# Six products for one extra row of a Fourier transform, with its low half in column 32 of the high operand; two real parts ahead in layer 0

## The chip, the cores and the metric

The kernel runs on one core of a Trainium2 chip. The metric is the device time of one launch in microseconds (us). A core has a matrix engine (TensorE, PE in the profile; PEld is its loading of the stationary operand), VectorE (DVE), ScalarE (ACT), GpSimd (POOL) and SyncE (SP, which here issues the DMAs). Each engine works off its own queue of instructions in order; engines wait for each other through semaphores.

## What is computed

Two layers, each a Fourier mixing and then a linear attention, both on the layer norm of the residual stream `x` (2048 tokens of 640, fp32):

```python
def _A_ref(x, dft_seq_re, dft_seq_im, dft_hid_re, dft_hid_im):
    a = jnp.einsum("bsd,ed->bse", x, dft_hid_re)
    b = jnp.einsum("bsd,ed->bse", x, dft_hid_im)
    y = jnp.einsum("ts,bse->bte", dft_seq_re, a) - jnp.einsum("ts,bse->bte", dft_seq_im, b)
    return y

def _B_ref(x, wqkv, wo):
    ...
    phi = lambda t: jnp.where(t > 0, t + 1, jnp.exp(t)) + 1e-6
    pq, pk = phi(q), phi(k)
    kv = jnp.einsum("bhsd,bhse->bhde", pk, v)
    z = jnp.einsum("bhsd->bhd", pk)
    num = jnp.einsum("bhqd,bhde->bhqe", pq, kv)
    den = jnp.einsum("bhqd,bhd->bhq", pq, z)[..., None] + 1e-6
    ...

x = x + _A_ref(_layernorm(x, axis=-1), ...)
x = x + _B_ref(_layernorm(x, axis=-1), B_wqkv, B_wo)
x = x + _A_ref(_layernorm(x, axis=-1), ...)
x = x + _B_ref(_layernorm(x, axis=-1), B_wqkv, B_wo)
```

There are 32 heads of width 20. The time depends on shapes alone.

## The kernel before

**Numbers in pairs.** TensorE multiplies here in fp32r, a rounded form of fp32. To keep fp32's precision, every operand is held as a pair: a high half (ScalarE casts it, L183) and a low half (the source minus the high half, L184, on VectorE or GpSimd). A product is then three: high by high, high by low, low by high.

**Fourier.** The transform over the sequence runs first, then the one over the channels. Both use the symmetry of the matrices, so that only real parts over 322 of the 640 channels and half of the sequence rows are multiplied; the rest are sums and differences. The sequence's results are kept by `kept` as pairs of 128x640 tiles, named `u` in the trace and `UT[ci, c]` in the code: `ci` 0 to 2 is the kind of transform, `c` 0 to 2 a chunk of 128 channels. Columns 0 to 511 of a tile are four groups of 128 sequence rows. For `ci == 0` there is one more sequence row, the middle one, t = 1024: column 512. The kernel fills the columns behind it with zeros, since the extra row is multiplied as a stationary operand of 128 columns.

`hidden` multiplies one group of 128 columns by the channel matrix: three chunks by three products, nine in all (L1102). `outputs(par, ahead, mid)` makes the residual's new rows: `par` 1 is the odd sequence rows, 0 the even ones. For each of four groups `r` there is a real part and an imaginary part in one psum buffer (names `ps`; there are four such buffers, and a product waits until the one it is given comes free). `ahead` says how many real parts stand ahead of the first imaginary part. When both parts of a group are done, ScalarE copies the imaginary part (L1129), VectorE makes difference `ym` and sum `yp` (L1130, L1131), and four additions put them into `x`: L1133 on VectorE and L1134 on GpSimd for the lower rows, L1141 and L1142 for the upper ones. In group 0 of the even rows, the extra row comes between: nine products into a psum buffer of its own, `p2`, and two copies (L1138, L1139) that put it into row 0 of `ym` and `yp`, after `ym`'s and `yp`'s old row 0 has been used by L1133 and L1134.

**What stands around it.** `PLANS` gives each layer its order: `o11 … w b q o03t` is, for layer 0, odd rows, sequence transforms, then the key projection's weights (`w`), the first normalized tile (`b`), the query projection's weights (`q`), and the even rows with three real parts ahead (`o03`). The `t` gives `outputs` a `mid` that is called once the first group's imaginary part is issued: it turns the first normalized tile by five transposes on TensorE (L196), into one psum buffer, and splits it (L183, L184). Behind the even rows stands the attention's first pass: the key and query projections (L245), a token tile at a time.

In layer 0 the weights come from memory: each of the 128x640 tiles is loaded by SP into one of four raw buffers, cast on ScalarE (L183) and subtracted (L184) on VectorE, or, for four of the five query tiles, on GpSimd. In layer 1 they are read back ready made. The scheduler sets the order of instructions on each engine, from the program's order, what depends on what, and a table of offsets (`AHEAD`); on each engine the instructions then run in that order.

Of the kernel before, what the change touches and what calls it, by code (L numbers as in the profile page):

```python
# [8 lines left out]
F32 = mybir.dt.float32  # L9
F32R = mybir.dt.float32r  # L10
AF = mybir.ActivationFunctionType
ALU = mybir.AluOpType
# [44 lines left out]
ASTATS = ((4, 10, 11, 13, 14), (1, 4, 8, 10))  # L57
VSTATS = ((4, 7, 13), (1, 2, 6, 7, 8, 13, 15))
RESID = ((4, 4), (3, 3))
PLANS = ('o11 s11 s12 s02 s00 s01 s10 w b q o03t', 's00 o12 s11 s12 s10 s01 s02 b w q o01t')  # L60
COL = (0, 1, 3, 2)
WLOWS = ((4, 0), (1, 1))
PAUSES = (4, 10, 11, 12, 13, 14)
# [955 lines left out]
class Fourier:  # L1019
# [58 lines left out]
    def kept(self, ci, pu, hi, lo, eng):  # L1078
        k, nc = self.k, self.k.nc
        if ci < 2:  # L1080
            woven = lambda t: t[:, :512].rearrange("p (n two) -> p two n", two=2)
            k.split(pu.rearrange("p (two n) -> p two n", two=2)[:, :, :256], woven(hi), woven(lo))
        else:
            nc.scalar.copy(hi[:, :512], pu)
            eng.tensor_tensor(lo[:, :512], pu, hi[:, :512].bitcast(F32), op=ALU.subtract)
        if ci == 0:
            for t in (hi, lo):
                nc.gpsimd.memset(t[:, 514:].bitcast(F32), 0.0)
            k.split(pu[:, 256:258], hi[:, 512:514], lo[:, 512:514])

    def whole(self, T, ci, c):
        pu = self.k.psum()
# [11 lines left out]
    def outputs(self, par, ahead, mid=None):  # L1104

        k, nc, X = self.k, self.k.nc, self.X
        pu = {}

        def real(r):
            if r < 4:  # L1110
                pu[r] = k.psum()
                self.hidden(2 * par, 128 * r, pu[r], 0)

        for r in range(ahead):
            real(r)
        for r in range(4):
            p = pu[r]
            self.hidden(2 * par + 1, 128 * r, p, 512)
            if r == 0 and mid is not None:
                mid()  # L1120
            g, q = 2 * par + r % 2, r // 2
            lo, hi = X[4 * g + q], X[4 * g + 3 - q]
            yi = k.temp(shape=(128, 322))
            ym, yp = k.temp(shape=(128, 322)), k.temp(shape=(128, 322))
            with k.ahead("out", par, r):
                if par:
                    nc.scalar.activation(yi, p[:, 512:834], AF.Copy, scale=k.sign[:, int(r in (1, 2)) :][:, :1])
                else:
                    nc.scalar.copy(yi, p[:, 512:834])  # L1129
                nc.vector.tensor_tensor(ym, p[:, :322], yi, op=ALU.subtract)  # L1130
                nc.vector.tensor_tensor(yp, p[:, :322], yi, op=ALU.add)  # L1131
            with k.ahead("lo", par, r):
                nc.vector.tensor_tensor(lo[:, :HC], lo[:, :HC], ym[:, :HC], op=ALU.add)  # L1133
                nc.gpsimd.tensor_tensor(lo[:, HC:], lo[:, HC:], yp[:, 1:HD], op=ALU.add)  # L1134
            if par == 0 and r == 0:
                p2 = k.psum()
                self.hidden(0, 512, p2, 0)
                nc.vector.tensor_copy(ym[0:1, :], p2[0:1, :322])  # L1138
                nc.vector.tensor_copy(yp[0:1, :], p2[0:1, :322])  # L1139
            with k.ahead("hi", par, r):  # L1140
                k.engine(r < RESID[k.layer][par]).tensor_tensor(hi[:, :HC], hi[:, :HC], yp[:, :HC], op=ALU.add)  # L1141
                nc.gpsimd.tensor_tensor(hi[:, HC:], hi[:, HC:], ym[:, 1:HD], op=ALU.add)  # L1142
            real(r + ahead)
# [17 lines left out]
    def run(self, T, att):  # L1161

        self.work(T, att, PLANS[self.k.layer])

# [370 lines left out]
```

## Time and profile before

| | us |
|---|---|
| median of 3 runs | 749.95 |
| lowest and highest | 749.91, 750.39 |
| profiled execution | 750.25 |
| its span, from first to last instruction | 748.1 |
| mean TensorE clock granted | 1.00 |

The profile is of one execution, on the one core. It is a page and views of its trace: the chain of waits follows the work that ended last back from the end, naming at each step what released it; a timeline gives an engine's instructions with start, duration, number and the idle time before (and what ended it); a group collects the instructions of one line, engine and form, with busy time, mean ns of one, and the idle time of the engine just before them. The names of tiles are written without their numbers. TensorE is busy 726.5 us of the span, VectorE 585.1, ScalarE 374.5, GpSimd 248.9.

Durations overlap a little: an instruction's row reaches into the start of the next of its engine.

### The profile page before, as it was taken

What the parts mean: (1) busy time and instruction counts of PE and PEld (TensorE: products, weight loads), DVE (VectorE), ACT (ScalarE), POOL (GpSimd) and SP (SyncE); (2) the same over time, 40 slices, a digit from 0 to 9 for tenths busy, and PEclk for the clock granted to TensorE, in tenths of its full rate; (3) what the DMA queues carried; (4) which work ended last, traced back from release to release, by engine and by line L of the source; (5) the groups of instructions that cost most, each with busy time, mean ns of one, the idle gap of its engine ahead of it and who ended that gap; (6) DMA issues with size and microseconds to landing.
All of it is one profiled execution on the core that took longest, in us unless ns stands there. A gap on an engine that the chain in (4) does not pass through costs nothing.

```text
span 748.1 us, 12737 instructions
## 1 busy us (share of the span) xinstructions
PE 726.5 (97%) x4734; PEld 690.3 (92%) x4734; DVE 585.1 (78%) x1142; ACT 374.5 (50%) x705; POOL 248.9 (33%) x282
## 2 busy tenths in 40 slices
PE   4999999999999999999999999999999999999997
PEld 1388999999999999899986999999999999989997
DVE  7997798758968786888984756966887886689983
ACT  7745655664355543455773336566532554443320
POOL 5237932120014002567773672026000020154300
PEclk9999999999999999999999999999999999999999
DMA  9322467445665840400043222645265535002553
GB/s 335 97 90 90 128 201 257 126 133 181 187 187 184 283 146 21 151 9 1 11 140 133 70 94 77 222 144 168 59 187 168 164 114 155 23 12 71 178 171 114
DMA packets 55548, 98.78 MB, mean 132 GB/s; under 512 B 5268, under 2 KB 22935, under 8 KB 55479
## 3 DMA queue, kind: packets, MB, share of 16 engines
q1 hardware_dynamic: 55479, 97.89, 41.2%
q8 instruction: 39, 0.64, 0.4%
q14 instruction: 30, 0.25, 0.1%
HBM read 75.84 MB, written 21.63 MB: 130 GB/s over the span
## 4 chain that ended last, share of the span: by engine, by line
PE 80%; DVE 10%; ACT 6%; issue 2%; DMA 1%; POOL 1%; SPq 0%; DVEq 0%; ACTq 0%
PE ps L245 50%; PE ps L338 18%; PE ps L1156 4%; PE ps L1102 4%; PE ps L520 2%; PE ps L196 1%; DVE t L184 1%; PE ps L1061 1%; DVE w L184 1%; ACT t L885 1%; DVE ps L586 1%; DVE x L615 1%; ACT t L886 1%; ACT ab L922 1%; ACT ab L923 1%
## 5 line engine op out<-in xcount | busy, mean ns | idle before, releaser
L245 PE MATMUL ps<-w,t 128*128 128x320 f32 x2880 | 432.4, 310 | 0.5 <-DVE w L184 0.2
L245 PEld LDWEIGHTS ps<-w,t 128*128 128x128 f32 x2880 | 422.9, 188 | 2.0 <-DVE t L184 0.4
L338 PE MATMUL ps<-t,t 128*128 128x256 f32 (+1 forms) x640 | 139.9, 309 | 0.0
L1230 DVE CUSTOM_DVE_ANT_0 junk<-ck,ck 128x688 bf16<-128x688 f32 (+5 forms) x138 | 103.6, 751 | 7.5 <-DMA ck<-in_ck 5.7
L338 PEld LDWEIGHTS ps<-t,t 128*128 128x128 f32 x640 | 106.9, 188 | 0.0
L338 PE MATMUL ps<-w,t 128*128 128x384 f32 (+1 forms) x320 | 98.6, 310 | 0.7 <-DVE w L184 0.6
L370 ACT ACTIVATE t<-ps 128x640 f32<-128x640 f32 x64 | 45.1, 704 | 96.3 <-PE ps L245 96.2
L183 ACT CAST t<-t 128x640 fp32r<-128x640 f32 x62 | 45.2, 728 | 68.7 <-DVE t L213 41.1
L570 POOL TENSOR_TENSOR t<-pq,t 128x640 f32<-128x640 f32 x26 | 42.5, 1642 | 106.4 <-ACT t L488 77.3
L407 POOL TENSOR_TENSOR t<-t,s 128x640 f32<-128x640 f32 x16 | 28.4, 1772 | 130.1 <-DVE s L373 123.5
L338 PEld LDWEIGHTS ps<-w,t 128*128 128x128 f32 x320 | 60.2, 188 | 1.4 <-DVE w L184 1.3
L184 DVE TENSOR_TENSOR t<-t,t 128x640 fp32r<-128x640 f32 x52 | 43.3, 833 | 19.5 <-ACT t L183 11.7
L1102 PE MATMUL ps<-t,u 128*128 128x322 f32 x306 | 48.1, 315 | 1.1 <-DVE t L184 1.1
L1102 PEld LDWEIGHTS ps<-t,u 128*128 128x128 f32 x306 | 46.0, 189 | 2.2 <-issue 1.3
L372 ACT ACTIVATE t<-t 128x640 f32<-128x640 f32 x64 | 47.5, 742 | 0.0
L373 DVE SCALAR_TENSOR_TENSOR pq<-t,pq 128x640 f32<-128x640 f32 x32 | 27.6, 863 | 23.9 <-ACT t L372 23.9
L373 DVE SCALAR_TENSOR_TENSOR s<-t,s 128x640 f32<-128x640 f32 x32 | 26.9, 842 | 20.4 <-ACT t L372 20.4
L184 POOL TENSOR_TENSOR t<-t,t 128x640 fp32r<-128x640 f32 x10 | 16.2, 1620 | 71.9 <-ACT t L183 71.8
L183 ACT CAST t<-ps 128x640 fp32r<-128x640 f32 (+1 forms) x36 | 24.8, 690 | 27.2 <-PE ps L196 23.5
L183 ACT CAST t<-s 128x640 fp32r<-128x640 f32 x32 | 23.3, 728 | 29.5 <-DVE t L184 17.4
L1156 PE MATMUL ps<-cw,ab 128*128 128x512 f32 x80 | 35.6, 595 | 1.4 <-ACT ab L922 1.0
L184 DVE TENSOR_TENSOR t<-ps,t 128x640 fp32r<-128x640 f32 (+1 forms) x36 | 29.2, 812 | 7.9 <-ACT t L183 7.9
(198 smaller groups left out, 987.3 us busy)
## 6 DMA issues: line engine op xcount, KB each, us to landing
ck<-in_ck SPq DMA_DIRECT2D x48, 346.0 KB
ck<-in_ck SPq DMA_DIRECT2D x48, 344.0 KB
turn<-t SPq DMA_DIRECT2D x23, 320.0 KB
save<-w SPq DMA_DIRECT2D x20, 320.0 KB
w<-save SPq DMA_DIRECT2D x20, 320.0 KB
z<-turn SPq DMA_DIRECT2D x19, 320.0 KB
x<-in_x SPq DMA_DIRECT2D x16, 320.0 KB
out<-x SPq DMA_DIRECT2D x13, 320.0 KB
```

Source lines behind the costliest of these rows:

```text
L183: self.nc.scalar.copy(hi, src)
L184: return self.engine(pool).tensor_tensor(lo, src, hi.bitcast(F32), op=ALU.subtract)
L245: nc.tensor.matmul(pu[:m, 512 * h : 512 * h + HD], s, w[:, HD * h : HD * h + HD], start=first, stop=last)
L338: nc.tensor.matmul(self.place(G, c, part), x[:, 128 * c : 128 * c + 128], p[:, f : f + n], start=start and i == 0, stop=stop and i == 2, s ...
L370: nc.scalar.activation(h2(e), halves(pu), AF.Relu, scale=-1.0)
L372: nc.scalar.activation(e, e, AF.Exp, scale=-1.0)
L373: k.ve.scalar_tensor_tensor(out, e, 1e-6, out, op0=ALU.add, op1=ALU.add)
L407: k.engine(n not in PKSUMS[k.layer]).tensor_tensor(pksum, pksum, pk, op=ALU.add)
L570: k.behind(k.nc.gpsimd.tensor_tensor(t1, self.PQ[self.order2[n]], self.zb, op=ALU.mult), lull)
L1102: self.k.nc.tensor.matmul(po[:, o : o + 322], s[:, f : f + 128], w[:, x, :], start=start, stop=stop)
L1156: self.k.nc.tensor.matmul(self.sum(j), T.out["o", q][:, 128 * j : 128 * j + 128], self.C[2, g], start=n == 0, stop=n == 3)
L1230: i = nc.vector.tensor_tensor_reduce(k.junk[:, : a.shape[1]], b, a, 1.0, 0.0, op0, op1, o)
```

## The change

One digit of a plan, and the extra row. In layer 0, two real parts stand ahead of the first imaginary part in the even rows, not three.

The extra row's column is now split into two columns of one tile: the high half into column 512 of the high tile, the low half into its column 544, that is column 32 of the 128 that the stationary operand takes. The columns between and behind are zeros, made by two memsets in the high tile; the low tile gets no memset. One product then gives, in row 0 of the psum buffer, the high half's result, and in row 32 the low half's, so two products for each chunk (high and low half of the channel matrix) do instead of three. The low half is multiplied by both halves of the matrix. The results are on different partitions: ScalarE copies row 32 to a one-row tile, and two additions on VectorE put the sum into row 0 of `ym` and `yp`, in place of two copies.

```diff
-PLANS = ('o11 s11 s12 s02 s00 s01 s10 w b q o03t', 's00 o12 s11 s12 s10 s01 s02 b w q o01t')
+PLANS = ('o11 s11 s12 s02 s00 s01 s10 w b q o02t', 's00 o12 s11 s12 s10 s01 s02 b w q o01t')
...
         if ci == 0:
-            for t in (hi, lo):
-                nc.gpsimd.memset(t[:, 514:].bitcast(F32), 0.0)
-            k.split(pu[:, 256:258], hi[:, 512:514], lo[:, 512:514])
+            for f, e in ((513, 544), (545, 640)):
+                nc.gpsimd.memset(hi[:, f:e].bitcast(F32), 0.0)
+            k.split(pu[:, 256:257], hi[:, 512:513], hi[:, 544:545])
...
             if par == 0 and r == 0:
-                p2 = k.psum()
-                self.hidden(0, 512, p2, 0)
-                nc.vector.tensor_copy(ym[0:1, :], p2[0:1, :322])
-                nc.vector.tensor_copy(yp[0:1, :], p2[0:1, :322])
+                p2, low = k.psum(), k.temp(shape=(1, 322))
+                for x in range(6):
+                    nc.tensor.matmul(
+                        p2[:, :322], self.UT[0, x // 2][0][:, 512:], self.hw[0, x // 2][:, x % 2, :], start=x == 0, stop=x == 5
+                    )
+                nc.scalar.copy(low, p2[32:33, :322])
+                nc.vector.tensor_tensor(ym[0:1, :], p2[0:1, :322], low, op=ALU.add)
+                nc.vector.tensor_tensor(yp[0:1, :], p2[0:1, :322], low, op=ALU.add)
```

In the new numbering the products are L1138, the copy of the low row L1141, the two sums L1142 and L1143, and the upper rows' additions L1145 and L1146 (L1141 and L1142 before). Over the program there are 4728 products instead of 4734.

Three engines' orders in layer 0 differ near the transposes of `mid`. First TensorE, from the transposes on: `ps_745`, `ps_755` and `ps_765` are the psum buffers of groups 0, 1 and 2 of the even rows, `ps_784` that of the transposes, `ps_802` the extra row's. Before, ahead of the transposes stand three real parts (27 products), the first imaginary part (9) and one product of the second:

```order
L1102 MATMUL ps_755<-t_386,u_644 128x322 x2
L1102 MATMUL ps_755<-t_386,u_645 128x322
L1102 MATMUL ps_755<-t_392,u_658 128x322 x2
L1102 MATMUL ps_755<-t_392,u_659 128x322
L1102 MATMUL ps_755<-t_380,u_630 128x322 x2
L1102 MATMUL ps_755<-t_380,u_631 128x322
L1102 MATMUL ps_765<-t_386,u_644 128x322 x2
```

This is the piece before where, in the changed order, the transposes stand (there `ps_774`; `ps_792` is the extra row's):

```order
L1102 MATMUL ps_755<-t_380,u_631 128x322
L196 MATMUL ps_774<-ident,t_705 128x128 x5
L1102 MATMUL ps_745<-t_426,u_671 128x322 x2
L1102 MATMUL ps_755<-t_426,u_671 128x322 x2
L1102 MATMUL ps_745<-t_426,u_672 128x322
L1102 MATMUL ps_745<-t_418,u_611 128x322 x2
L1102 MATMUL ps_745<-t_418,u_612 128x322
L1102 MATMUL ps_745<-t_447,u_620 128x322 x2
L1102 MATMUL ps_745<-t_447,u_621 128x322
L1138 MATMUL ps_792<-t_386,u_644 128x322 x2
L1138 MATMUL ps_792<-t_392,u_658 128x322 x2
L1138 MATMUL ps_792<-t_380,u_630 128x322 x2
```

The transposes now stand behind two real parts (18 products), and the extra row's six products right behind the first imaginary part; before, its nine stood behind three real and three imaginary parts. From the transposes to the third real part it is 24 products. The psum buffer that `ps_802` took was the one that the transposes' split gives back; `ps_792` takes one that is idle, and the third real part takes the transposes' one.

Second, ScalarE. `w` are weight tiles cast from a raw tile out of memory, `t_790<-ps_784` (now `t_780<-ps_774`) is the cast of the transposes, `ps_745` and `ps_755` the copies of the first two imaginary parts. Before:

```order
L183 CAST w_695<-raw_693 128x640
L183 CAST w_701<-raw_699 128x640
L183 CAST w_717<-raw_715 128x640
L183 CAST t_790<-ps_784 128x640
L183 CAST w_723<-raw_721 128x640
L1129 COPY t_794<-ps_745 128x322
L183 CAST w_729<-raw_727 128x640
L1129 COPY t_835<-ps_755 128x322
```

And now:

```order
L183 CAST w_695<-raw_693 128x640
L183 CAST t_780<-ps_774 128x640
L183 CAST w_701<-raw_699 128x640
L1129 COPY t_784<-ps_745 128x322
L183 CAST w_717<-raw_715 128x640
L1141 COPY t_793<-ps_792 1x322
L183 CAST w_723<-raw_721 128x640
L1129 COPY t_824<-ps_755 128x322
```

The cast of the transposes has moved ahead of the casts `w_701` and `w_717`, and the first imaginary part's copy ahead of `w_717`; the new copy of the low row stands behind `w_717`.

Third, GpSimd, from its first weight split on. `x_98` is the tile to which L1134 adds `yp` of group 0, `x_104` and `x_112` take upper rows. Before:

```order
L184 TENSOR_TENSOR w_718<-raw_715,w_717 128x640
L184 TENSOR_TENSOR w_724<-raw_721,w_723 128x640
L184 TENSOR_TENSOR w_730<-raw_727,w_729 128x640
L1134 TENSOR_TENSOR x_98<-x_98,t_796 128x319
L184 TENSOR_TENSOR w_736<-raw_733,w_735 128x640
```

And now:

```order
L184 TENSOR_TENSOR w_718<-raw_715,w_717 128x640
L1134 TENSOR_TENSOR x_98<-x_98,t_786 128x319
L184 TENSOR_TENSOR w_724<-raw_721,w_723 128x640
L1146 TENSOR_TENSOR x_104<-x_104,t_785 128x319
L184 TENSOR_TENSOR w_730<-raw_727,w_729 128x640
L184 TENSOR_TENSOR w_736<-raw_733,w_735 128x640
```

Group 0's additions have moved in among the weight splits: L1134 stands behind one of them instead of three.

## The prediction, made before the changed kernel was run

> **What bounds the kernel now.** I read the page first, for the engine that is never idle.
>
> ```profile
> span 748.1 us, 12737 instructions
> PE 726.5 (97%) x4734; PEld 690.3 (92%) x4734; DVE 585.1 (78%) x1142; ACT 374.5 (50%) x705; POOL 248.9 (33%) x282
> PE 80%; DVE 10%; ACT 6%; issue 2%; DMA 1%; POOL 1%; SPq 0%; DVEq 0%; ACTq 0%
> L1102 PE MATMUL ps<-t,u 128*128 128x322 f32 x306 | 48.1, 315 | 1.1 <-DVE t L184 1.1
> ```
>
> TensorE is busy for 97% of the span and carries 80% of the chain that ended last, so a product taken away is worth its own time, and so is a stall of PE. The last row is the group that the change thins out: 306 products of L1102, and the only idle time ahead of them is 1.1 us behind a split on VectorE. Where that stands among PE's waits, the second view tells (columns: total us, times, longest us).
>
> ```profile
> PE ps L779 <- DMA x<-in_x: 11.0, 1, 11.0
> PE ps L245 <- DVE t L184: 1.9, 3, 1.5
> PE ps L1102 <- DVE t L184: 1.1, 1, 1.1
> ```
>
> After the first load, PE's longest waits are of 1.5 and 1.1 us; the second is the one ahead of L1102. Third, the weight loads of PE in layer 0 (start, duration, count), which mark the products' own times better than the pipelined matmul ends.
>
> ```profile
> 63.63 5.64 PEld L1102 LDWEIGHTS ps<-t,u 128*128 128x128 f32 x37
> 69.24 0.62 PEld L196 LDWEIGHTS ps<-ident,t 128*128 128x128 f32 x5
> 69.82 2.54 PEld L1102 LDWEIGHTS ps<-t,u 128*128 128x128 f32 x17
> 73.66 4.06 PEld L1102 LDWEIGHTS ps<-t,u 128*128 128x128 f32 x27 [1.29 <-issue]
> 77.90 2.21 PEld L245 LDWEIGHTS ps<-w,t 128*128 128x128 f32 x15 [0.18 <-ACT t L1129]
> ```
>
> The even output rows of layer 0 run from 63.63 to 77.90, 14.27 us for 81 products and 5 transposes. Idle in it are 1.29 and 0.18, together 1.47. The transposes take 69.82 − 69.24 = 0.58. The loads add up to 5.64 + 2.54 + 4.06 = 12.24 us, 0.151 each. Fourth, the chain of waits says what the 1.29 hung on.
>
> ```profile
> 66.57 0.83 DVE w L184
> ...
> 67.41 3.93 DMA raw<-in_wqkv
> ...
> 71.36 0.02 ACT w L183
> ...
> 72.00 0.70 ACT t L183
> ...
> 72.72 0.84 DVE t L184
> ...
> 73.69 4.29 PE ps L1102 x27
> ```
>
> The transposes were done at 69.9, but their cast (ACT t L183) stands in ScalarE's queue behind a cast of a weight tile that came from memory at 71.36. So the cast ran at 72.00, the split's second half on VectorE at 72.72, and only then was the transposes' psum buffer free for the extra row's products at 73.69. PE's stall is a DMA's lateness, handed on by the order of ScalarE's queue.
>
> **The change part by part.** *Three products fewer in each layer.* 3 × 0.151 = 0.45 us in layer 0, on the path, since PE is.
>
> *The stall in layer 0.* With two real parts ahead, the transposes stand after 18 products instead of 37, and their cast ahead of two casts that wait for memory, not behind both. Whether the stall goes is a walk with these rows (ScalarE and VectorE, layer 0):
>
> ```profile
> 64.55 2.61 ACT L183 CAST w<-raw 128x640 fp32r<-128x640 f32 x4
> 69.72 0.73 ACT L183 CAST w<-raw 128x640 fp32r<-128x640 f32 x1 [2.57 <-DMA raw<-in_wqkv]
> 65.83 3.02 DVE L184 TENSOR_TENSOR w<-raw,w 128x640 fp32r<-128x640 f32 x4
> 73.21 0.43 ACT L1129 COPY t<-ps 128x322 f32<-128x322 f32 x1
> 73.67 0.49 DVE L1130 TENSOR_TENSOR t<-ps,t 128x322 f32<-128x322 f32 x1
> 72.17 4.86 POOL L184 TENSOR_TENSOR w<-raw,w 128x640 fp32r<-128x640 f32 x3 [3.98 <-DMA raw<-in_wqkv]
> 76.99 1.12 POOL L1134 TENSOR_TENSOR x<-x,t 128x319 f32<-128x319 f32 x1
> ```
>
> Real parts end at 63.63 + 18 × 0.151 = 66.35, transposes at 66.93. The cast can follow the four casts that end at 67.16 and ends at 67.9 (0.70); VectorE's four splits end at 68.85, the transposes' split at 69.7. The psum buffer that it frees is wanted by the third real part, 24 products behind the transposes, at 66.93 + 3.62 = 70.55: 0.85 to spare. The extra row's own buffer is an idle one. The fourth real part, at 73.27, wants the buffer of the first, which L1131 frees: cast of a weight 69.72 to 70.45, copy L1129 to 70.9, a weight's split to 71.3, two sums of 0.49 that overlap by a little to 72.2: 1.1 to spare. So both stalls go, 1.47, and key projection starts at 63.63 + 78 × 0.151 + 0.58 = 75.99, 1.91 earlier than 77.90.
>
> *A new wait.* The key projection's first psum buffer is now the extra row's, free after L1143. That sum writes row 0 of the tile that GpSimd's L1134 reads, so it waits for L1134; L1134 stands in GpSimd's queue behind one weight split (72.17, 4.86 / 3 = 1.62 each, to 73.8), and takes 1.12, to 74.9; then L1143 to 75.4. That is 0.6 ahead of 75.99. Queued behind L1143 on VectorE are the next row's L1130 and L1131, which free psum buffers of projections behind the first.
>
> *Small parts.* GpSimd issues two memsets a tile where it issued two (one in each tile of the pair then, both in the high one now), on its queue ahead of the normalization's powers:
>
> ```profile
> L1088 POOL MEMSET u<- x6: 202/203/212, 62.6 to 64.5; 128x126 f32 x6
> 64.64 0.61 DVE L177 TENSOR_SCALAR t<-x,kept 128x640 f32<-128x640 f32 x1 [0.65 <-POOL kept L158]
> ```
>
> Narrower ones of 31 and 95 columns should cost no more than 0.20 each and no less than nothing; should their place in the queue cost VectorE's L177 one of them, all times of the walk are 0.2 later and each margin above 0.2 smaller, none below zero. I count nothing. The new ScalarE copy L1141 (one row of 322 columns) lies between nothing and the 0.43 of L1129, which has as many columns on 128 rows; I take the upper. L1142 and L1143 replace copies of the same width, 0.48 by L1139's row further down; I take that. ScalarE's waits for memory (2.57 in the row above) and PE's products hide L1141; were the cover gone, 0.43 once in a layer.
>
> *What PE keeps of 1.91.* An engine that doesn't get earlier can take it back. GpSimd is that one.
>
> ```profile
> 80.00:100.00 20.00, 20.00 (x140) 20.00 (x139) 15.11 (x31) 12.93 (x21) 19.83 (x27) 1.00 0.27 79
> 97.42 0.92 ACT L171 ACTIVATE t<-x,nb,kept 128x640 f32<-128x640 f32 x1 [2.81 <-POOL nb L168]
> 101.02 24.16 PE L245 MATMUL ps<-w,t 128*128 128x320 f32 x163
> 103.81 0.82 DVE L184 TENSOR_TENSOR t<-ps,t 128x640 fp32r<-128x640 f32 x1
> 134.88 0.83 DVE L373 SCALAR_TENSOR_TENSOR pq<-t,pq 128x640 f32<-128x640 f32 x1 [3.80 <-ACT t L372]
> ```
>
> The first row is the busy time by stretch (PE, its loads, VectorE, ScalarE, GpSimd): from 80 to 100 GpSimd is busy 19.83 of 20.00, and its work starts with the DMA at 72.17 and is the same as before. It hands out the scales of the first normalized tiles, and ScalarE's normalization at 97.42 waited 2.81 for one. That tile's transposes are split by 103.81 + 0.82 = 104.63, and its low half is read first by the 38th product of the stretch from 101.02: 101.02 + 37 × 24.16 / 163 = 106.5, 1.9 to spare. PE 1.91 earlier wants it at 104.6. So PE keeps all but some 0.0 to 0.2; with a split of an earlier tile about as close, I take off 0.2. From 130 on VectorE waits for ScalarE, which waits for PE (3.80 in the last row), so what PE has kept until then it keeps. Layer 0: 1.91 − 0.2 = **1.7**.
>
> *Layer 1.* One real part ahead as before; three products fewer, no stall to remove:
>
> ```profile
> 427.11 11.63 PEld L1102 LDWEIGHTS ps<-t,u 128*128 128x128 f32 x78
> 438.70 7.38 PEld L245 LDWEIGHTS ps<-w,t 128*128 128x128 f32 x50
> 447.68 2.51 PEld L245 LDWEIGHTS ps<-w,t 128*128 128x128 f32 x17 [0.17 <-ACT t L183]
> 432.12 1.05 POOL L1134 TENSOR_TENSOR x<-x,t 128x319 f32<-128x319 f32 x1 [7.67 <-DVE t L1131]
> 433.20 0.48 DVE L1139 COPY t<-ps 1x322 f32<-1x322 f32 x1 [0.18 <-POOL x L1134]
> ```
>
> 3 × 11.63 / 78 = 0.45. But PE's next small wait (0.17 at 447.68) hangs on additions that GpSimd begins at 432.12, and these wait for the first imaginary part, ahead of which few of the lost products stand. If they move by two products, 0.30 is kept, if by three, 0.45. I take **0.4**.
>
> The sum is 1.7 + 0.4 = 2.1. The profiled execution took 750.25, 2.15 around its span of 748.1, which I leave as it is; the median of the three runs, 749.95, is 0.30 below it. The change gives 749.95 − 2.1 = **747.85**.
>
> *A rule that speaks against it.* Beside GpSimd, VectorE's additions are slow: L1133 took 1.12 in layer 0 and 0.48 with GpSimd's queue less full:
>
> ```profile
> 74.48 1.12 DVE L1133 TENSOR_TENSOR x<-x,t 128x321 f32<-128x321 f32 x1
> 431.95 0.48 DVE L1133 TENSOR_TENSOR x<-x,t 128x321 f32<-128x321 f32 x1
> ```
>
> The Trainium skill, page "SBUF — State Buffer", section "Who interferes with whom", has the reason as an exclusive lock: a VectorE instruction with two operands in SBUF and a GpSimd instruction that reads SBUF shut each other out for a whole instruction. By that rule an addition of VectorE that now falls onto GpSimd's first splits would push GpSimd back by its 0.48, and the total would be some 1.6, the time 748.3; by the rows alone GpSimd's time is unchanged and it stays 747.85. The two rows agree with the rule's direction.
>
> **The rivals.** *GpSimd keeps the gain.* GpSimd's order changes too: two additions (L1134, L1146) move in among the weight splits. A fourth split, alone among additions, has taken longer than the 1.62 of the three:
>
> ```profile
> 78.07 2.17 POOL L184 TENSOR_TENSOR w<-raw,w 128x640 fp32r<-128x640 f32 x1
> ```
>
> If all three take 2.17, GpSimd is 3 × 0.55 = 1.65 later at the normalization scales; the low half of 104.63 comes at 106.3 where PE wants it at 104.6, and PE loses 1.7 of its 1.91. Layer 0 gives 0.2, layer 1 0.4, at worst 749.35; with half of that lag, 0.8, it is 748.6. For it speaks the stretch with 19.83 of 20.00; against it that VectorE's additions are as many as before. The likely place is **749.1**, which is also what three products in each layer give with no help from the stall (749.95 − 0.9 = 749.05): the rival that the move of the transposes does nothing.
>
> *VectorE's queue is caught behind GpSimd: slower.* L1143 waits for L1134, L1134 for a weight split, and that split for a tile from memory. Before, the first split's tile came at 71.36 (its cast), and it started at 72.17. From a start later than 72.8, L1143 ends after 75.99 and PE waits one for one: a start at 74.9 eats up all 2.1. What would make it late is the DMA: the raw buffers are given back by casts and splits, which now stand behind L1129 and the extra row. If one such transfer has to be waited for, 3.93 as in the chain, L1143 ends at 79.3, PE loses 3.3 of it, and the change costs 3.3 − 2.1 = 1.2; if the buffer comes free a split (1.62) later besides, 2.9. Between them lies **752.0**. Against it speaks that the first split's tile is on its way from 67.41, on a buffer that VectorE's split of 66.57 gives back, and that split stands ahead of all that is moved.
>
> **How the numbers follow.** The likeliest case, that both stalls go and GpSimd takes back little, I give 0.66; its own range is 747.2 (nothing taken back, 1.47 + 0.9 = 2.37, and the spread of some tenths between runs) to 748.4. GpSimd keeps the gain: 0.24, at 748.4 to 749.6. The caught queue: 0.10. The range 747.2 to 749.6 takes the first two in and leaves out the third. A measurement of this kernel can tell about 0.2%, 1.5 us, from no change: faster is below 748.45, slower above 751.45. Nearly all of the first case is faster, most of the second is within 0.2%, and the third is mostly slower: 0.66, 0.26, 0.08.
>
> **What would show it.** Right: 4728 matmuls, 288 on L1102 and 12 on L1138; no wait of L1102 behind VectorE's t L184; key projection of layer 0 about 1.9 earlier from the even rows' start; L1143 idle behind GpSimd's L1134 for a few tenths; a small PE wait on a split's low half at about 104; layer 1's 11.63 down to some 11.2; a span near 746.0. Wrong: PE waiting at the key projection behind L1143, GpSimd's splits at 2.2 each, or a new wait behind GpSimd in the first projections. If the products still to do were granted a lower clock than the 1.00 of the stretch above, the whole sum would be off.

## The result, and the profile after

The changed kernel takes 748.18 us (median of 8 runs, 747.26 to 749.35); runs of the kernel before beside it gave 750.2 (749.22 to 752.0). The ratio is 0.9975, with a 95% interval of 0.9964 to 0.9986. The profiled execution took 747.7, its span is 745.6. The prediction was 747.85, with a range of 747.2 to 749.6. Against the prediction's own mark of 0.2%, the gain of 0.25% counts as faster by the median, but the interval, 0.14% to 0.36%, spans that mark.

The page of the changed kernel, in the lines that answer to those shown of before:

```profile
span 745.6 us, 12728 instructions
PE 725.7 (97%) x4728; PEld 689.3 (92%) x4728; DVE 589.0 (79%) x1142; ACT 375.2 (50%) x707; POOL 246.8 (33%) x282
PE 77%; DVE 12%; ACT 4%; DMA 4%; issue 2%; POOL 1%; SPq 1%; DVEq 0%; ACTq 0%
L1102 PE MATMUL ps<-t,u 128*128 128x322 f32 x288 | 45.6, 315 | 0.0
```

The products are 4728, and ahead of L1102 PE no longer idles (1.1 before). But the chain that ended last runs less through PE (80% before) and more through VectorE and DMA (10% and 1% before): a second chain has come to light. PE's waits (total, times, longest) name its end:

```profile
PE ps L779 <- POOL qve L904: 10.7, 1, 10.7
PE ps L245 <- DVE t L184: 1.9, 3, 1.5
...
PE ps L196 <- DVE t L177: 0.2, 1, 0.2
```

The wait of L1102 is gone; new is one of transposes (L196) behind a normalization on VectorE (L177). The weight loads of PE in layer 0 (start, duration, count) give the amounts:

```profile
63.30 2.80 PEld L1102 LDWEIGHTS ps<-t,u 128*128 128x128 f32 x18
66.06 0.62 PEld L196 LDWEIGHTS ps<-ident,t 128*128 128x128 f32 x5
66.66 1.64 PEld L1102 LDWEIGHTS ps<-t,u 128*128 128x128 f32 x11
68.26 0.94 PEld L1138 LDWEIGHTS ps<-t,u 128*128 128x128 f32 x6
69.16 6.48 PEld L1102 LDWEIGHTS ps<-t,u 128*128 128x128 f32 x43
75.60 6.17 PEld L245 LDWEIGHTS ps<-w,t 128*128 128x128 f32 x42
...
98.61 0.53 PEld L196 LDWEIGHTS ps<-ident,t 128*128 128x128 f32 x5 [0.44 <-PE ps L245]
```

The even rows take 75.60 − 63.30 = 12.30 us without an idle moment, 1.97 less than the 14.27 of before. Then, from the key projection's start to the transposes of tile 3, it is 98.61 − 75.60 = 23.01 us. Before it was 22.52, from 77.90 to the second of these rows of before; the first is tile 3's normalization on VectorE:

```profile
97.86 0.60 DVE L177 TENSOR_SCALAR t<-x,kept 128x640 f32<-128x640 f32 x1
...
100.42 0.61 PEld L196 LDWEIGHTS ps<-ident,t 128*128 128x128 f32 x5
```

And the normalization of the changed kernel:

```profile
97.91 0.59 DVE L177 TENSOR_SCALAR t<-x,kept 128x640 f32<-128x640 f32 x1
```

In time from the span's start it has stayed where it was, while PE came 2 us earlier: it used to end 2.0 ahead of the transposes, and now they wait for it. So 0.49 of the 1.97 is given back there, most of it in the idle time of 0.44.

Counted from the even rows' start, L177 begins after 34.61 us, 0.38 later than before (34.23). Ahead of it in VectorE's queue stands the work on tile 2. L213, which takes that tile from memory, is 0.24 earlier by this count (25.13 for 25.37), but the split behind it (L184) takes 0.86 longer. Here it is with the GpSimd instruction that overlaps it, before and then after:

```profile
91.21 1.21 DVE L184 TENSOR_TENSOR t<-t,t 128x640 fp32r<-128x640 f32 x1 [0.21 <-ACT t L183]
91.69 2.19 POOL L407 TENSOR_TENSOR t<-t,s 128x640 f32<-128x640 f32 x1
```

```profile
89.86 2.16 POOL L407 TENSOR_TENSOR t<-t,s 128x640 f32<-128x640 f32 x1
90.63 2.07 DVE L184 TENSOR_TENSOR t<-t,t 128x640 fp32r<-128x640 f32 x1
```

GpSimd's L407 has come 1.50 earlier by the same count (26.56 for 28.06), so it now starts ahead of the split and not behind it; kernel 8 below takes this overlap up. By these rows, an estimate: with a split of 1.21 again, L177 would come 0.86 earlier, and PE would not have waited in this execution. No kernel here tests that alone.

The lengths of these two stretches, **even rows** and **key projection to tile 3**, measure all that follows. In layer 1:

```profile
425.29 0.45 PEld L1102 LDWEIGHTS ps<-t,u 128*128 128x128 f32 x3
...
436.41 7.41 PEld L245 LDWEIGHTS ps<-w,t 128*128 128x128 f32 x50
```

The stretch took 11.12, where it took 11.59 (427.11 to 438.70): 0.47 less. Added up against the profile of before, PE is 0.33 ahead at the even rows of layer 0 (the first load of `x` came earlier, nothing of the change), 2.30 at the key projection, 1.81 at tile 3, 1.82 at layer 1's even rows, 2.29 behind them, and 2.5 at the end.

Two rows each of GpSimd and VectorE show the walk of the prediction as it came out:

```profile
70.94 1.59 POOL L184 TENSOR_TENSOR w<-raw,w 128x640 fp32r<-128x640 f32 x1 [4.00 <-ACT w L183]
72.47 1.14 POOL L1134 TENSOR_TENSOR x<-x,t 128x319 f32<-128x319 f32 x1
...
73.64 0.48 DVE L1143 TENSOR_TENSOR t<-ps,t 1x322 f32<-1x322 f32 x1 [0.18 <-POOL x L1134]
```

GpSimd's first split starts at 70.94, not at the 72.17 of before, and L1143 ends at 74.1, 1.5 ahead of the key projection.

### The profile page after: what moved, and what is told of

It reads as the page before. It is cut to its first block, busy times and chain, and to the rows that moved or that the text cites. A ratio compares the mean times of both kernels' runs of the same rounds, so it can differ in the third digit from the quotient of the medians.

```text
span 745.6 us, 12728 instructions
## 1 busy us (share of the span) xinstructions
PE 725.7 (97%) x4728; PEld 689.3 (92%) x4728; DVE 589.0 (79%) x1142; ACT 375.2 (50%) x707; POOL 246.8 (33%) x282
## 4 chain that ended last, share of the span: by engine, by line
PE 77%; DVE 12%; ACT 4%; DMA 4%; issue 2%; POOL 1%; SPq 1%; DVEq 0%; ACTq 0%
PE ps L245 47%; PE ps L338 18%; PE ps L1160 4%; PE ps L1102 3%; DMA x<-in_x 2%; PE ps L520 2%; DVE t L184 2%; PE ps L196 1%; PE ps L1061 1%; DVE w L184 1%; DVE ps L586 1%; DVE x L615 1%; DMA raw<-in_wqkv 1%; DVE t L593 1%; ACT ab L922 1%
## 5 line engine op out<-in xcount | busy, mean ns | idle before, releaser
L245 PE MATMUL ps<-w,t 128*128 128x320 f32 x2880 | 432.3, 310 | 0.5 <-DVE w L184 0.2
L245 PEld LDWEIGHTS ps<-w,t 128*128 128x128 f32 x2880 | 422.9, 188 | 1.9 <-DVE w L184 0.4
L183 ACT CAST t<-t 128x640 fp32r<-128x640 f32 x62 | 45.2, 728 | 73.9 <-DVE t L213 46.3
L407 POOL TENSOR_TENSOR t<-t,s 128x640 f32<-128x640 f32 x16 | 28.0, 1752 | 126.4 <-DVE s L373 119.9
L184 DVE TENSOR_TENSOR t<-t,t 128x640 fp32r<-128x640 f32 x52 | 45.1, 868 | 18.8 <-ACT t L183 10.9
L1102 PE MATMUL ps<-t,u 128*128 128x322 f32 x288 | 45.6, 315 | 0.0
L1102 PEld LDWEIGHTS ps<-t,u 128*128 128x128 f32 x288 | 43.3, 189 | 0.9 <-ACT u L1084 0.4
L184 POOL TENSOR_TENSOR t<-t,t 128x640 fp32r<-128x640 f32 x10 | 16.2, 1619 | 72.1 <-ACT t L183 72.1
L183 ACT CAST t<-ps 128x640 fp32r<-128x640 f32 (+1 forms) x36 | 24.9, 691 | 27.9 <-PE ps L196 24.5
L183 ACT CAST t<-s 128x640 fp32r<-128x640 f32 x32 | 23.3, 727 | 29.6 <-DVE t L184 17.6
L158 POOL TENSOR_TENSOR kept<-ve,mhalf 128x1 f32<-128x1 f32 x32 | 21.9, 706 | 40.5 <-DVE ve L157 39.3
```

The lines of the kernel that those rows point to most:

```text
L183: self.nc.scalar.copy(hi, src)
L184: return self.engine(pool).tensor_tensor(lo, src, hi.bitcast(F32), op=ALU.subtract)
L245: nc.tensor.matmul(pu[:m, 512 * h : 512 * h + HD], s, w[:, HD * h : HD * h + HD], start=first, stop=last)
L407: k.engine(n not in PKSUMS[k.layer]).tensor_tensor(pksum, pksum, pk, op=ALU.add)
L1102: self.k.nc.tensor.matmul(po[:, o : o + 322], s[:, f : f + 128], w[:, x, :], start=start, stop=stop)
```

## The experiments

No kernel here leaves a part of the computation out. The ratio is to runs of the kernel before beside it. Each line of the table is one series of runs; its last two columns (us) are from the execution that was profiled.

| kernel | median us (range, runs) | ratio, 95% interval | even rows | key to tile 3 |
|---|---|---|---|---|
| before | 750.2 (749.22 to 752.0, 8) | | 14.27 | 22.52 |
| changed | 748.18 (747.26 to 749.35, 8) | 0.9975 [0.9964, 0.9986] | 12.30 | 23.01 |
| changed, again | 748.17 (747.48 to 749.52, 9) | 0.9973 [0.9962, 0.9983] | 12.29 | 24.02 |
| 1 plan only | 746.9 (746.38 to 748.22, 6) | 0.9957 [0.9943, 0.9971] | 12.74 | 22.75 |
| 1 plan only, again | 747.69 (747.42 to 748.05, 5) | 0.9965 [0.9951, 0.9978] | 12.74 | 22.90 |
| 2 six products only | 748.87 (748.0 to 751.49, 12) | 0.9985 [0.9975, 0.9996] | 13.52 | 22.50 |
| 3 transposes first | 749.82 (747.98 to 754.38, 12) | 1.0003 [0.9986, 1.002] | 13.56 | 23.03 |
| 4 statistics behind tile 3 | 750.27 (749.0 to 751.04, 12) | 0.9995 [0.9985, 1.0004] | 12.33 | 23.69 |
| 5 fewer of them | 748.49 (747.46 to 748.89, 10) | 0.9976 [0.9967, 0.9985] | 12.35 | 24.02 |
| 6 six in layer 1 only | 746.89 (746.86 to 747.39, 5) | 0.9956 [0.9943, 0.997] | 12.75 | 22.51 |
| 6 again | 747.3 (746.89 to 748.25, 6) | 0.9963 [0.9949, 0.9978] | 12.75 | 22.80 |
| 7 own buffers | 748.38 (747.79 to 749.9, 12) | 0.9979 [0.997, 0.9988] | 12.30 | 23.01 |
| 8 own buffers, six in layer 1 only | 747.98 (746.91 to 749.1, 11) | 0.9973 [0.9964, 0.9982] | 12.75 | 23.42 |
| 9 turn ahead of the check | 747.24 (747.03 to 747.79, 5) | 0.9964 [0.9951, 0.9978] | 12.29 | 22.51 |

**1. The plan alone.** Nine products, two real parts ahead:

```diff
-PLANS = ('o11 s11 s12 s02 s00 s01 s10 w b q o03t', ...
+PLANS = ('o11 s11 s12 s02 s00 s01 s10 w b q o02t', ...
```

> The kernel before with two real parts ahead in layer 0; the extra row still takes nine products. Theory (the stall hung on the order of ScalarE's queue, so moving the transposes takes it away by itself): the 1.29 and 0.18 us of idle in the even rows are gone, key projection of layer 0 starts 12.8 us after the even rows' start instead of 14.3, and as PE is then 0.45 later than in the changed kernel, the wait at the next transposes but one (0.44 there) is nearly gone: 1.4 to 1.5 us faster than before, ratio about 0.998. Rival (the gain is the products that are not done, the plan does nothing): within 0.2 us of before, key projection 14.3 after the start.

> The plan alone once more. The products of its first profile followed each other every 147.71 ns on average, those of the changed kernel every 147.87: over 4700 of them 0.75 us that no wait explains. Theory (that was the execution, not the kernel): 1.4 to 1.6 us faster than before, ratio 0.998, spacing back at 147.85. Rival (it is the kernel's own): ratio 0.9957 again, spacing 147.7.

```profile
66.36 9.43 PEld L1102 LDWEIGHTS ps<-t,u 128*128 128x128 f32 x63
75.75 6.17 PEld L245 LDWEIGHTS ps<-w,t 128*128 128x128 f32 x42
```

In the first execution, 63 products run without a break, and the even rows take 12.74: the stall, 14.27 − 12.74 = 1.53, is gone by the plan alone. The time was expected 1.4 to 1.5 below the kernel before, and came 3.1 and 2.3 below it. Neither expectation has this: both medians, 746.9 and 747.69, lie below the changed kernel's, which has six products fewer.

**2. The six products alone** (the changed kernel with `o03t`).

> The changed kernel with three real parts ahead in layer 0, as before: only the six products. Theory: the stall stays, the extra row still waits for the transposes' psum buffer at 10.0 us after the even rows' start, and PE gains 3 x 0.15 in each layer, 0.9 us in all, ratio about 0.9988. Rival (GpSimd and VectorE hold what PE gains): 0.3 us or less.

```profile
72.74 0.90 PEld L1138 LDWEIGHTS ps<-t,u 128*128 128x128 f32 x6 [0.20 <-issue]
...
74.48 2.69 PEld L1102 LDWEIGHTS ps<-t,u 128*128 128x128 f32 x18 [0.85 <-ACT w L183]
```

Of the stall 1.05 stays, behind the cast of a weight tile. The even rows gain 0.75, and the key projection is late enough that nothing is given back by tile 3 (22.50). The median is 1.1 below the kernel before beside it (749.97), for the 0.9 expected.

**3. The transposes first.** The kernel before, nine products and `o03t`, with `mid` ahead of the first imaginary part:

```diff
+        if mid is not None:
+            mid()
         for r in range(4):
...
-            if r == 0 and mid is not None:
-                mid()
```

> The kernel before, three real parts ahead and nine products, but the transposes stand between the real parts and the first imaginary part, after 27 products instead of 37, so that their cast stands ahead of the one weight cast that waited longest for memory. Theory (a late DMA handed on by ScalarE's order): the cast ends near 71, the psum buffer is free at 72.2 where PE wants it at 72.4, the 1.29 us of idle goes to 0.0 to 0.2: 1.1 to 1.4 us faster than before. Rival (what helps is a psum buffer more, since two real parts take one less): the buffer is as scarce as before, so the stall stays within 0.3 of its 1.29 and the time is that of before.

```profile
68.62 7.78 PEld L1102 LDWEIGHTS ps<-t,u 128*128 128x128 f32 x51
77.04 6.12 PEld L245 LDWEIGHTS ps<-w,t 128*128 128x128 f32 x42 [0.63 <-issue]
```

The cast ran at 70.27, and the idle 1.29 ahead of the extra row is gone, as the chain of before says it should. But PE then stood idle 0.63 at the key projection and another 0.48 before tile 3, and the time is that of before, where 1.1 to 1.4 less was expected. To remove a stall is not to gain it.

**The changed kernel again**, for a second profile.

> The changed kernel itself, beside the plan-only kernel on the same chip. Theory (six products in layer 0 are worth 0.45 us at the key projection, but PE gives 0.4 of it back at the transposes of token tile 3; those of layer 1 are worth 0.45): 2.0 us faster than before, ratio 0.9973, and 0.4 to 0.6 us faster than the plan alone. Rival (the plan alone is the better kernel, since GpSimd's and ScalarE's orders around the extra row suit it better): the plan alone stays ahead by 1 us.

```profile
85.21 1.18 PEld L245 LDWEIGHTS ps<-w,t 128*128 128x128 f32 x8 [0.44 <-ACT t L183]
86.73 12.04 PEld L245 LDWEIGHTS ps<-w,t 128*128 128x128 f32 x82 [0.33 <-DVE t L184]
99.44 0.53 PEld L196 LDWEIGHTS ps<-ident,t 128*128 128x128 f32 x5 [0.67 <-PE ps L245]
```

Here 1.50 is given back, at tile 1's cast, its low half and tile 3's transposes. The first weight tile that casts wait for was cast 6.7 us after the even rows' start, 5.9 in the other execution: what comes from memory hands its lateness on. The time was expected 0.4 to 0.6 below that of the plan alone; beside it, it is 0.5 above (748.17 against 747.69).

**4 and 5. Statistics held behind tile 3** (changed kernel). Ahead of L177 of tile 3 VectorE does statistics of tiles that are needed much later. Those of tiles 7 and up (then 12 and up) are held behind it:

```diff
-            nc.vector.bn_stats(st[:, 0, :], x[:, :HD])
+            self.behind(nc.vector.bn_stats(st[:, 0, :], x[:, :HD]), self.hold)
...
+        self.k.hold = self.k.gate if n >= 7 and not self.k.layer else None
...
+        self.k.gate = done if n == 3 else self.k.gate
```

> The changed kernel with one order more: in layer 0 the statistics of token tiles 7 and on are held on VectorE until the normalization of token tile 3 (L177) is done, so that it comes about 2 us earlier. Theory (what layer 0 loses behind the even rows is VectorE's queue: statistics stand ahead of a normalization whose transposes PE waits for): PE's idle of 0.44 ahead of the transposes at 98.6 goes, 0.35 to 0.45 us faster than the changed kernel, about 747.8. Rival (the prediction's: GpSimd's scales are what is late): VectorE's earlier place doesn't help, the same 0.4 us is lost at those transposes or at a split's low half some us later.

> The changed kernel with the normalization of token tile 3 held ahead of the statistics of token tile 12 and on (not 7 and on): on VectorE it moves past two or three statistics alone, some 0.4 us, and ScalarE's and GpSimd's orders stay. Theory: PE's idle of 0.44 ahead of that tile's transposes falls to 0.0 to 0.1 and nothing later is delayed: 0.3 to 0.4 us faster than the changed kernel. Rival (what is late comes from the DMA of the weights, not from VectorE's order): no change within 0.2, the wait moves with the landing of the weight tiles.

Both expectations, a gain of some tenths, missed. In the first PE came to tile 3 without waiting, yet the kernel was 2.1 slower than the changed one: the held statistics came too late for later tiles. PE's weight loads there stood idle for 1.07 behind ACT t L183 at 123.6, and for 0.81 and 0.89 behind POOL t L184 at 125.6 and 134.7; in the second form they don't. Both forms waited at tile 1 already (0.83 and 0.32; 0.82 and 0.31). The milder form gained nothing. In both executions the weight tiles came late (first cast 7.2 us after the even rows' start), so 23.69 and 24.02 don't measure the edit alone.

**6. Six products in layer 1 only** (two real parts ahead; layer 0 keeps nine).

```diff
-        if ci == 0:
+        if ci == 0 and not k.layer:
+            for t in (hi, lo):
+                nc.gpsimd.memset(t[:, 514:].bitcast(F32), 0.0)
+            k.split(pu[:, 256:258], hi[:, 512:514], lo[:, 512:514])
+        elif ci == 0:
```

and likewise in `outputs`.

> Two real parts ahead in layer 0; nine products for the extra row in layer 0, six in layer 1. Theory: layer 0 as with the plan alone (1.4 to 1.5 us), layer 1 the 0.45 of three products: 1.9 us, within 0.1 of the changed kernel. Rival (three products in layer 0 are worth their own time): 0.45 slower than the changed kernel.

> The same kernel as the run with six products in layer 1 alone (746.89), once more beside the two with other buffers. If the layer 0 version with nine products is really better than the change: 746.9 to 747.4, below the changed kernel's 748.2 again. If its first run was drawn from the good end of a spread that both share: 747.8 or more.

746.89 and 747.3: below the changed kernel twice, which neither expectation of the first run has. The five runs of the first series (up to 747.39) all lie below the nine of the changed kernel beside them (from 747.48). In layer 0 six products instead of nine bring 0.45 at the key projection (12.30 against 12.75) and nothing that lasts; tile 3 isn't ready for them.

**7. Own buffers.** In the changed kernel ScalarE's second normalization (tile 2) waited 3.54 for an L1131 to release a temporary. Tiles 1 and 2 of layer 0 get buffers of the weights' pool:

```diff
-        xn = self.k.temp()
+        xn = self.k.wp.tile([128, 640], F32, tag="w", name=...) if n in (1, 2) and not self.k.layer else self.k.temp()
```

> The changed kernel, with nothing left out; the normalized tiles 1 and 2 of layer 0 (L171) get buffers of the weights' pool in place of two of the rotating temporaries. ScalarE's second L171 then no longer waits for the third of VectorE's L1131 (3.54 us in the changed kernel's profile, 3.80 in its second one); VectorE's and GpSimd's orders stay as they are, and nothing else moves but ScalarE's copy of the last extra group. Theory A (what the changed kernel gives back behind the key projection starts at that buffer): the second L171 follows the first directly, about 15 us after the even rows' start in place of 17.9 to 18.7; VectorE's transposition L213 starts 1 to 2.5 us earlier (24.8 or less in place of 25.1 to 26.3); PE's waits at tile 1's cast (0.44 in the second profile) and before the transposes of tile 3 (0.44 and 0.67) are gone, and the kernel takes 0.4 to 1.0 less than the changed one: 747.2 to 747.8. Theory B (what is given back hangs on when the weights land and on VectorE's own order of statistics): L171 moves but L177 of tile 3 does not, the waits stay, 748.2. Theory C (the two early normalizations push ScalarE's copy L1129 of the last extra group, hence VectorE's and GpSimd's additions, back by 1.8): tile 1's low half or the transposes come later, 748.5 or more.

The normalization was done by 78.11, 4 us earlier, and nothing followed from it: theory A, which I held, fell; L177 begins 34.60 after the even rows' start (34.61 without the buffers), as theory B has it. The chain of waits of this kernel (start, duration, what) shows why:

```profile
77.79 2.19 POOL w L184
79.97 0.02 issue
79.99 0.33 SPq L1209
80.32 0.05 issue
80.37 5.29 DMA turn<-xn
85.66 0.02 issue
85.67 2.68 DMA z<-turn
...
88.45 1.35 DVE t L213
...
98.06 0.53 DVE t L177
98.58 0.14 issue
98.72 0.74 PE ps L196 x5
```

Read upward: tile 3's transposes wait for its normalization; that stands on VectorE behind statistics and, ahead of these, L213, which takes tile 2 turned through memory; the turn was issued at 80.37, directly behind the last of four check transfers (L1209) on SyncE's queue, of 346 KB each; and this waited for a raw buffer that a GpSimd split gave back. From 80 to 86 the DMA engines were 73% busy, and the turn took 5.29 beside the check transfers, where in the changed kernel it took 2.74, issued 1.7 later (82.11, when the buffer had come free). Both ways `z` lands at the same time, so either gate alone hides behind the other.

**8. The same with nine products in layer 0.**

> Nine products in layer 0 with the plan of the change, six in layer 1 (as in the run with six products in layer 1 alone), and the buffers of the weights' pool for the normalized tiles 1 and 2. Here L171 waited 2.25 for VectorE's L1135, and the profile showed no wait of PE before the transposes of tile 3. Theory A: nothing is waiting there, so nothing is gained: 746.9, within 0.4. Theory B: the same, 746.9. Theory C: 747.2 or more.

The time is one that theory C allows, but not by its reason: the additions that it speaks of came 0.2 later against the even rows' start, the last three 0.8 later, not 1.8. `z` landed as without the buffers (L213 25.98 us after the even rows' start; 25.95 in the second profile of kernel 6), but PE waited 0.91 before tile 3. Between the two profiles differs VectorE's split behind L213; with the buffers, then without:

```profile
90.51 2.15 POOL L407 TENSOR_TENSOR t<-t,s 128x640 f32<-128x640 f32 x1
91.27 2.08 DVE L184 TENSOR_TENSOR t<-t,t 128x640 fp32r<-128x640 f32 x1
```

```profile
90.44 1.55 POOL L407 TENSOR_TENSOR t<-t,s 128x640 f32<-128x640 f32 x1
92.60 0.81 DVE L184 TENSOR_TENSOR t<-t,t 128x640 fp32r<-128x640 f32 x1
```

Beside GpSimd's L407 it takes 2.08 and ends 0.7 behind it; begun after L407, 0.81. The Trainium skill, page "SBUF — State Buffer", section "Who interferes with whom", calls the port pair that the two share an exclusive lock; 92.66 (L407's end) + 0.81 = 93.47 against the measured end 93.35 agrees within 0.12. The buffers aren't needed for the overlap: the split takes 2.02 in the first profile of kernel 6, without them, and 2.07 and 1.93 in the two of the changed kernel. Whether they make it more frequent is open, and the ranges of 8 and 6 overlap.

**9. The turn ahead of the check** (changed kernel, buffers of 7). Layer 0's first check transfers are asked for behind the first tile's feed:

```diff
-        if check is not None:
+        if check is not None and k.layer:
             check.fetch()
...
-                        if check is not None and check.more:
+                        if check is not None and (not n and not k.layer or n and check.more):
                             check.fetch()
```

On SyncE the turn and `z` now stand ahead of four L1209; the other engines keep their orders.

> The changed kernel with the two buffers of the run before (tiles 1 and 2 of layer 0 normalized into the weights' pool), and with the first four check transfers (L1209, 346 KB each) issued on SyncE behind the turn of tile 2 (L204, L208) in place of ahead of it. Nothing is left out, and the other engines keep their orders. In the run with the buffers alone, L171 was done by 78.1 but the turn was issued at 80.4, directly behind the check transfers, and took 4.9 us beside them, so that z landed when it did in the changed kernel (L213 25.07 after the even rows' start, 25.13 there). Theory D (tile 3 is late because tile 2's turn stands behind the check transfers on SyncE's queue and shares the DMA engines with them): the turn is issued at about 78.2, L213 starts 2 to 3 us earlier (22 to 23 after the even rows' start, then bound by VectorE's low half of tile 1), L177 of tile 3 follows 1.5 to 3 earlier, PE's wait before the transposes of tile 3 (0.44 to 0.91) is gone, and layer 0's six products are kept at last: 747.2 to 747.8. Theory E (tile 3's normalization hangs on something else in VectorE's queue, such as the statistics' own inputs from GpSimd's additions): L213 moves, L177 does not, the wait stays, 748.2. Theory F (the check transfers land late for VectorE's L1217 and L1234 at 100, and push tile 3's low half): the wait before tile 3's transposes goes and another comes behind L184 at 103: 748.2 or more.

Its timeline, SyncE first, then VectorE and PE:

```profile
79.11 0.39 SPq L204 DMA_DIRECT2D turn<-xn  x1
82.01 0.34 SPq L208 DMA_DIRECT2D z<-turn  x1
82.44 1.80 SPq L1209 DMA_DIRECT2D ck<-in_ck  x4
...
85.24 1.35 DVE L213 STREAM_TRANSPOSE t<-z 128x640 f32<-128x640 f32 x1
...
96.91 0.60 DVE L177 TENSOR_SCALAR t<-x,kept 128x640 f32<-128x640 f32 x1
...
98.34 0.61 PEld L196 LDWEIGHTS ps<-ident,t 128*128 128x128 f32 x5
```

Theory D holds in its direction: L213 is 3.4 earlier against the even rows' start (21.70; 25.13 in the changed kernel), L177 1.2, where 1.5 to 3 was expected, since VectorE then waited 1.79 for GpSimd; PE comes to tile 3 without a wait, 22.51 behind the key projection, the length of before. The weights don't explain it: the first late cast lay 5.8 to 5.9 after the even rows' start here, in kernel 7 and in the changed kernel's first profile. The median is 747.24, every run of it below 747.8. The medians of kernels 1, 6 and 9 all lie below those of the kernel before and of the changed one; among themselves their ranges overlap, and the intervals of their ratios overlap that of the changed kernel, so which is best is not settled. The order of transfers without the buffers, and with kernel 6, wasn't tried.

## Why the prediction was right, and where not

- *Three products fewer*: 0.45 in layer 0, measured 12.74 − 12.30 = 0.44 (kernel 1 against the changed one).
- *The stall in layer 0*: 1.47 by the walk, 1.53 by kernel 1. The chain of before was read rightly: kernels 1 and 3 both take the transposes' cast out from behind the late weight tile, and the 1.29 goes in both. Key projection came 1.97 earlier, for 1.91.
- *A new wait*: L1143 waits for L1134 as foretold (0.18), with 1.5 to spare instead of 0.6. The walk held GpSimd's first split at 72.17; it came at 70.94.
- *What PE keeps of 1.91*: **this step failed**, in place and cause. I took 0.2 off for tile 3's low half at 104, and read ScalarE's row at 97.42 as its normalization. That row is tile 4's; tile 3's is VectorE's L177 at 97.86, and its transposes, not its low half, wait first. I had looked at the engine with the fullest stretch, GpSimd, as the one that doesn't get earlier; it came 1.5 earlier, and in the changed kernel it idled 0.89 at 92.91 waiting for VectorE. What doesn't get earlier with PE is tile 2. Its way through memory stands behind the check transfers: L213 begins 25.13 and 26.26 after the even rows' start in the two executions, 25.37 before. And its split on VectorE takes 0.86 and 0.72 longer, beside GpSimd's L407. Kernel 9 shows the first part: it differs from 7 in SyncE's order alone, and PE's wait is gone. The second part is read from the rows and not tested alone. Together they take 0.49 of the 1.97 in one execution; in the other, with waits at tile 1 besides, 1.50 goes. Layer 0 kept 1.48 in the profile, for 1.7.
- *Layer 1*: 0.47 for 0.4; the small wait behind it stayed (0.16).
- *The sum*: 2.1 foretold; the medians are 2.0 apart. In the profile its terms come to 1.97 − 0.49 + 0.47 = 1.95; the rest of the span's 2.5 is the start (0.33) and 0.2 behind layer 1's even rows. Had the profile fallen on the second execution, with 1.50 given back, they would be 0.9. So it is partly luck that the total came this near: the step that failed allowed 0.2 for what was 0.49 and 1.50, and the 0.33 of the start has nothing to do with the change.
- *The exclusive lock* gave 748.3, close to the time, but that is luck, since its cause didn't occur: GpSimd's splits came earlier, not 0.48 later. Where the two engines overlapped, VectorE was the one held: L1133 took 1.40 beside GpSimd's first split (1.12 before), and L184 2.07 beside L407.
- *GpSimd keeps the gain*: its splits took no longer, so it fell as told. But there is a grain of it in kernel 7's chain, where a GpSimd split frees the raw buffer that the check transfer ahead of the turn needs. *VectorE's queue caught behind GpSimd* didn't happen.

Left open: the two lengths don't explain the medians to the last half microsecond. Kernel 9 is at tile 3 after 12.29 + 22.51 = 34.80, kernel 6 after 35.26 and 35.55, and yet it isn't faster (747.24 against 746.89 and 747.3); kernel 1, without the 0.47 of layer 1, took 746.9 in its first series. What goes with it is the mean spacing of PE's consecutive projection products (L245, start to start; of 2842 distances the 2835 to 2840 under 300 ns): 147.65 to 147.74 ns in kernels 1 and 6, 147.82 to 147.94 in all others, the kernel before among them (147.88). Over 4700 products that would be 0.4 to 1.4 us, an estimate. No run here tells its cause.

## What to carry to other kernels

A gain on the bounding engine ends at the next tile that doesn't get earlier with it: look for that tile by following each of the next few tiles back through its own chain, its transfers and the queue they are issued on included, not by looking for the fullest engine. Ask too whether an engine that does get earlier now starts ahead of one that doesn't, and holds it up. Then a transfer that is needed soon belongs ahead of bulk transfers that can wait, on the queue and on the DMA engines both. Where two edits are worth the same stretch, measure each alone: here one of them gained nothing in layer 0 until the next wait was out of the way.

## What the runs showed of the hardware

- The same kernel's weight tiles land at different times: the first late cast lay 5.9 and 6.7 us after the even rows' start in two executions of the changed kernel, 7.2 in kernels 4 and 5. The runs of the changed kernel, where PE waits at the end of that chain, spread over 2 us (747.26 to 749.35), and the five of kernel 9, where it doesn't, over 0.8. That the one comes of the other isn't shown: the kernel before doesn't wait there either, and spreads over 2.8.
- A turn of 320 KB, issued behind 1.4 MB of check transfers, took 5.29 us where 2.74 had done, so issuing it 1.7 earlier brought nothing.
- VectorE's 128x640 split took 0.81 us begun after GpSimd's L407 (kernel 6's second profile), and in the changed kernel and kernels 7 and 8 it took 1.9 to 2.1 begun beside it, ending about 0.7 behind it.
